# Loading q two groups ahead, and summing later key tiles on VectorE, in a fused attention and gate kernel

## The chip, the cores and the metric

The kernel runs on one core of one Trainium2 chip. The metric is the device time of one execution in microseconds (us). Three runs of the kernel before took 1133.68, 1138.77 and 1144.32 us; the median is 1138.77 us.

## The reference

Four batches (B = 4) of 12288 queries with C = 128 channels attend to 768 keys. The keys are a 4 x 4 mean over a 384 x 32 image, multiplied by `w_sr`; they serve as values too. The result goes through a five-tap causal convolution that makes a gate, and through two 128 x 128 products.

```
kv_pool = kv.reshape(B, H // r, r, W // r, r, C).mean(axis=(2, 4))     # r = 4
k = v = kv_pool.reshape(B, -1, C) @ w_sr                               # 768 keys a batch
a = softmax(q @ k.T / sqrt(C))                                         # 12288 x 768 a batch
x = a @ v
gate = sigmoid(sum over 5 taps of conv_w[k] * x shifted by 4 - k)
out = (gate * (x @ w_val)) @ w_out
```

## The kernel before

The 12288 queries of a batch are cut into 24 **groups** of 512 queries, 96 groups in all, and a group into 4 **steps** of 128 queries (j = 0 to 3). The schedule is written out by hand: one loop over all 384 steps emits, step by step, what each engine is to do, and each engine runs its instructions in that order. Work on a group is spread over several groups of the loop: at group gi the loop does the scores of gi (one step ahead), the product with the values ("AV") of gi - 2 (`avg`), the convolution of gi - 3 (`xg`) and the two last products of gi - 4 (`mg`).

What one step puts on each engine, with the lines of the profile:

- TensorE (PE): six matmuls of scores for the next step (L262); a part of the 18 AV matmuls of `avg` (L344), cut by `AV_CUTS`; at j = 0 the turning of the row sums (L290, into the tile `m`, of which there is one buffer); at j = 1 the product with `w_val` (L400, into `m` too); at j = 2 the product with `w_out` (L410); at j = 3 six transposes of the probabilities (L310), which need the tile `pf` from ScalarE.
- VectorE (DVE): the row maximum (L268), the low half of the probabilities of the step before (`p_lo`, L331); at j = 0 the reciprocal (L287); at j = 1 the copy `r` of the turned row sums (L297) and `h` (L405); at j = 3 `x` (L361), which scales AV by the row sums `rb`.
- ScalarE (ACT): the exponential (L280), the high half of the probabilities (L327), one tap of the convolution, a tanh, a copy out, and at j = 2 the rounded query `qh` (L244) of group gi + 2.
- GpSimd (POOL): the query's remainder `ql` (L248), four taps (L371) and four sums (L380) of the convolution.
- SyncE (SP) issues nearly all DMAs from one queue in order: the transposing DMAs that bring the probabilities of steps 0 to 2 from `hl` to `pt` (L335), the store `rd` (L298) and the broadcast load `rb` (L303) of the row sums, the query loads (L233), the output stores (L424).

The scores of a step lie in a pair of PSUM banks, `s`; there are three pairs, so the scores written at the end of a group (those for j = 0 of the next group) take the pair that `p_lo` of step j = 1 leaves.

Queries come in pairs of groups, into a tile `q` with two buffers. The pair gi + 2, gi + 3 is loaded at j = 0 of an even gi, and `qh` of gi + 2 is asked for at j = 2 of the same group.

Keys of the first batch come in 16 pieces of 48 keys (`load_kv`, L118) into `kvt`, and VectorE sums each (`pool_kv`, L123). The keys of the other batches are made while the batch before them is worked on, one small job a group (`setup_steps`, run at j = 3). There a half of the keys is 4 loads of 768 KB to the same tile, `rows`: a plain one from SP (L131) and three from GpSimd's queue that add to what is there (L133). VectorE then sums four neighbours in four instructions (`pool_rows`, L138), each in the group after its job, at j = 0, between `p_lo` and the next row maximum. Then come two projections, the scaling of the values and their splitting, in seven more jobs.

Of the kernel before, what the change touches and what calls it, by code (L numbers as in the profile page):

```python
# [6 lines left out]
F32 = mybir.dt.float32  # L7
F32R = mybir.dt.float32r
F16 = mybir.dt.float16
I32 = mybir.dt.int32  # L10
AF = mybir.ActivationFunctionType
ALU = mybir.AluOpType
AX = mybir.AxisListType
PSUM = bass.MemoryType.PSUM

R = 4
# [11 lines left out]
def attn_moe_kernel(ctx, tc, qT, kvT, w_sr, w_moe, outT):  # L28


    nc = tc.nc
    B, C, N = qT.shape
    NK, RR = kvT.shape[3] // R, R * R
    NCH = NK // P
    HALF = NK // 2
    NG = N // GQ
    NW = w_moe.shape[1]
    TAPS = NW - 2 * C
    HALO = TAPS - 1
    PIECES = 16  # L40
    AV_CUTS = (0, 7, 10, 14, 18)
    assert 3 * NCH == AV_CUTS[-1]
    PC = NK // PIECES
    QC = NK // 4
    scale = 1.0 / float(C) ** 0.5

    const = ctx.enter_context(tc.tile_pool(name="const", bufs=1))
    kvp = ctx.enter_context(tc.tile_pool(name="kvp", bufs=4))
# [25 lines left out]
    def load_moe():  # L74

        if w_moe.dtype == F32:
            nc.sync.dma_start(out=wm, in_=w_moe)
            return []
        raw = kvp.tile([C, HALF * R], F32, name="rows0", bufs=1).bitcast(I32)[:, :2 * NW]
        rest = kvp.tile([C, HALF * R], F32, name="rows1", bufs=1)  # L80
        nc.sync.dma_start(out=raw, in_=w_moe.bitcast(I32))
        words = raw.rearrange("c (n w) -> c w n", w=2)
        lo, hi = words[:, 0], words[:, 1]
        sign, ex, a, t = (rest.bitcast(I32)[:, i * NW:(i + 1) * NW] for i in range(4))
        low = rest[:, 4 * NW:5 * NW]
        v = nc.vector

        def two(out, in_, s1, op0, s2, op1):
            return lambda: v.tensor_scalar(out=out, in0=in_, scalar1=s1, scalar2=s2,
                                           op0=op0, op1=op1)  # L90

        def one(out, in_, s1, op):
            return lambda: v.tensor_single_scalar(out=out, in_=in_, scalar=s1, op=op)

        def both(out, x, y, op):
            return lambda: v.tensor_tensor(out=out, in0=x, in1=y, op=op)

        return [
            two(ex, hi, 20, ALU.logical_shift_right, 0x7FF, ALU.bitwise_and),
            two(ex, ex, -896.0, ALU.add, 0.0, ALU.max),  # L100
            two(ex, ex, 255.0, ALU.min, float(1 << 23), ALU.mult),
            two(a, hi, 0xFFFFF, ALU.bitwise_and, 3, ALU.logical_shift_left),
            two(t, lo, 29, ALU.logical_shift_right, 7, ALU.bitwise_and),
            both(a, a, t, ALU.bitwise_or),
            one(a, a, 0x3F800000, ALU.bitwise_or),
            one(sign, hi, -2147483648, ALU.bitwise_and),
            both(a, a, sign, ALU.bitwise_or),
            one(t, lo, 0x1FFFFFFF, ALU.bitwise_and),
            two(low, t, 2.0 ** -52, ALU.mult, 0.0, ALU.add),
            both(low.bitcast(I32), low.bitcast(I32), sign, ALU.bitwise_or),  # L110
            both(low, low, a.bitcast(F32), ALU.add),
            both(wm, low, ex.bitcast(F32), ALU.mult),
        ]

    def load_kv(st, i):
        t = kvp.tile([C, R, PC * R], F32, name="kvt", bufs=5)
        src = kvT[0].rearrange("r c x -> c r x")
        nc.sync.dma_start(out=t, in_=src[:, :, i * PC * R:(i + 1) * PC * R])  # L118
        st["kv", i] = t

    def pool_kv(st, i):
        t = st.pop(("kv", i))
        nc.vector.tensor_reduce(out=st["pool"][:, i * PC:(i + 1) * PC],  # L123
                                in_=t.rearrange("c r (k s) -> c k r s", s=R),
                                axis=AX.XY, op=ALU.add)

    def load_rows(b, st, h, r):
        src = kvT[b, r, :, h * HALF * R:(h + 1) * HALF * R]
        if r == 0:
            st["rows", h] = kvp.tile([C, HALF * R], F32, name=f"rows{h}", bufs=1)  # L130
            nc.sync.dma_start(out=st["rows", h], in_=src)  # L131
        else:
            nc.gpsimd.dma_start(out=st["rows", h], in_=src, accum_op=ALU.add)  # L133

    def pool_rows(st, i):
        t = st["rows", i // 2].rearrange("c (k s) -> c k s", s=R)
        k0 = i % 2 * QC
        nc.vector.tensor_reduce(out=st["pool"][:, i * QC:(i + 1) * QC], in_=t[:, k0:k0 + QC],  # L138
                                axis=AX.X, op=ALU.add)

    def key_tiles(st):
        st["pool"] = keys.tile([C, NK], F32, name="pool", bufs=1)
        for n in ("kh", "kl"):
            st[n] = keys.tile([C, NK], F32R, name=n)
        for n in ("vh", "vl"):
            st[n] = keys.tile([P, NK], F16, name=n)
        st["vt"] = keys.tile([C, NK], F32, name="vt", bufs=1)
# [67 lines left out]
                lambda: values(st, 1, misc()) or split_values(st, 1)]  # L215

    def setup_steps(b, st):
        loads = [(h, r) for r in range(1, R) for h in range(2)]
        steps = [lambda: key_tiles(st) or load_rows(b, st, 0, 0) or load_rows(b, st, 1, 0)]
        for h, r in loads:  # L220
            steps += [lambda: None, lambda h=h, r=r: load_rows(b, st, h, r)]
        steps += [lambda i=i: (None, lambda: pool_rows(st, i)) for i in range(4)]
        steps += [lambda h=h: project(st, h, misc()) or split_keys(st, h) for h in range(2)]
        return steps + value_steps(st)

# [214 lines left out]
    def at(i):  # L440
        return groups[i] if 0 <= i < G else None

    ctx.enter_context(tc.manual_schedule())
    st = states[0]
    key_tiles(st)
    for i in range(5):
        load_kv(st, i)
    load_second = load_pair(at(0), at(1), parts=2)
    nc.sync.dma_start(out=wsr, in_=w_sr)
    g_qh(at(0))  # L450
    g_ql(at(0))
    low = None
    for i in range(PIECES):
        if i + 5 < PIECES:
            load_kv(st, i + 5)
        if i == 3:
            convert = load_moe()
        pool_kv(st, i)
        if i >= 8 and convert:
            convert.pop(0)()  # L460
        if i == 3 * PIECES // 4:
            low()
        if i % (PIECES // 2) == PIECES // 2 - 1:
            h = 2 * i // PIECES
            project(st, h, bank_pair()[:, 0])
            high, low = split_keys(st, h)
            high()
    low()
    load_second()
    score(at(0), 0)  # L470
    g_qh(at(1))
    g_ql(at(1))

    steps = value_steps(st)
# [6 lines left out]
    for t in range(NT * G):  # L481
        gi, j = divmod(t, NT)
        cur, prev, nxt = (at(u // NT) for u in (t, t - 1, t + 1))
        last, avg, xg, mg, og = (at(gi - d) for d in (1, 2, 3, 4, 5))
        if j == 0 and gi % 2 == 0 and at(gi + 2):
            load_pair(at(gi + 2), at(gi + 3))
        if gi % NG == 1 and j == 0 and at(gi + NG - 1):
            steps += setup_steps(cur.b + 1, states[cur.b + 1])
        if t == NT + 2:
            trickle += convert  # L490

        if nxt:
            score(nxt, (j + 1) % NT)
        if mg and j == 1:
            mg.m = g_val(mg, misc())
        if mg and j == 2:
            mg.m = g_out(mg.h, misc())
        if avg:
            av_part(avg, j)

        if high and (j == 0 or t < NT):
            high()
            high = None
        row_max(cur, j)
        expo(cur, j)
        if on_pe(j):
            turn(cur, j)
            norm_eps(cur)
            if mg:
                out_tile(mg)  # L510
                g_evac(mg, mg.m)
        p_hi(cur, j)
        if mg and j == 0:
            mg.th = g_tanh(mg.gate)
        if xg and j == 1:
            tap(xg, TAPS - 1, nc.scalar)
        if last and j == 0:
            norm_reciprocal(last)
        if last and j == 1:
            norm_store(last)  # L520
        drip()
        if prev:
            p_lo(prev, (j - 1) % NT)
        if low and (j == 0 or t < NT):
            low()
            low = None
        if last and j == 0:
            norm_turn(last, misc())
        drip()
        if mg and j == 1:  # L530
            mg.h = g_h(mg.th, mg.m)
        if avg and j == 3:
            new_x(avg, xg, nc.gpsimd.tensor_copy)
            g_x(avg, avg.av)
        if xg and j == 1:
            g_conv(xg)
        if last and j == 3:
            norm_rows(last)
        if at(gi + 2) and j == 2:
            g_qh(at(gi + 2))  # L540
            g_ql(at(gi + 2))
        if og and j == 0 and og.i % 2:
            store_pair(og)
        if steps and (j == 3 or t < NT):
            high, low = steps.pop(0)() or (None, None)
# [83 lines left out]
```

## Time and profile before

| | |
|---|---|
| median of three runs | 1138.77 us (1133.68 to 1144.32) |
| the profiled execution's own time | 1141.0 us |
| its span, first to last instruction | 1139.2 us |
| granted TensorE clock, mean | 0.992 |
| busy: PE, DVE, ACT, POOL | 1059.9, 895.8, 909.0, 879.5 us |
| DMA queues' packets, share of 16 engines | q1 (from SP) 83.6%, q0 (from GpSimd) 7.7% |

The span is what the trace covers; the 1.8 us around it belong to the execution's own time. In rows of the profile, `out<-in` names the tiles, `x` the number of instructions, and what stands in brackets is the idle time of that engine just before, with the instruction that ended it. "L310 x6" are the six transposes at the end of a group, so the time from one such row to the next is the time of one group. "PEld" is TensorE's weight load, "SPq" an instruction of the SP queue. A busy PE is counted from modelled ends of pipelined matmuls: busy time there isn't time in which nothing more would fit.

### The profile page before, as it was taken

What the parts mean: (1) busy time and instruction counts of PE and PEld (TensorE: products, weight loads), DVE (VectorE), ACT (ScalarE), POOL (GpSimd) and SP (SyncE); (2) the same over time, 40 slices, a digit from 0 to 9 for tenths busy, and PEclk for the clock granted to TensorE, in tenths of its full rate; (3) what the DMA queues carried; (4) which work ended last, traced back from release to release, by engine and by line L of the source; (5) the groups of instructions that cost most, each with busy time, mean ns of one, the idle gap of its engine ahead of it and who ended that gap; (6) DMA issues with size and microseconds to landing.
All of it is one profiled execution on the core that took longest, in us unless ns stands there. A gap on an engine that the chain in (4) does not pass through costs nothing.

```text
span 1139.2 us, 16531 instructions
## 1 busy us (share of the span) xinstructions
PE 1059.9 (93%) x5174; PEld 711.9 (62%) x5174; DVE 895.8 (79%) x1254; ACT 909.0 (80%) x1659; POOL 879.5 (77%) x966
## 2 busy tenths in 40 slices
PE   1889999999999989999999999899999999999996
PEld 0656666666666656666666666566666666666663
DVE  6877777888877767788888787688887888778784
ACT  1777888888887878788888788788888888888882
POOL 0178888888878878887888898788887888888872
PEclk9999999999999999999999999999999999999999
DMA  8599999998989999989879999999798888878973
GB/s 269 99 229 186 213 195 229 187 181 184 188 200 203 219 178 204 197 180 190 177 161 226 226 212 216 178 210 185 155 176 191 176 172 193 189 160 183 197 148 107
DMA packets 489783, 215.53 MB, mean 189 GB/s; under 512 B 452704, under 2 KB 461664, under 8 KB 489696
## 3 DMA queue, kind: packets, MB, share of 16 engines
q1 hardware_dynamic: 487104, 200.32, 83.6%
q0 software_dynamic: 2592, 14.16, 7.7%
q8 instruction: 41, 0.67, 0.2%
q14 instruction: 46, 0.38, 0.1%
HBM read 75.83 MB, written 25.36 MB: 89 GB/s over the span
## 4 chain that ended last, share of the span: by engine, by line
PE 39%; DMA 23%; DVE 13%; ACT 12%; POOL 8%; issue 3%; SPq 2%; DVEq 0%; ACTq 0%; POOLq 0%
DMA q<-in_q 16%; PE s L262 14%; PE av L344 13%; DMA rb<-rd 6%; PE m L400 5%; DVE nm L268 5%; POOL tap L371 4%; PE s L310 4%; POOL ql L248 3%; ACT qh L244 3%; ACT s L280 3%; DVE x L361 3%; ACT pf L280 3%; ACT hl L327 2%; PE m L410 2%
## 5 line engine op out<-in xcount | busy, mean ns | idle before, releaser
L380 POOL TENSOR_TENSOR sum<-sum,tap 128x512 f32<-128x512 f32 x282 | 359.6, 1275 | 22.1
L344 PE MATMUL av<-pt,vh 128*128 128x512 f16 x1140 | 359.7, 384 | 9.3 <-DVE x L361 9.3
L268 DVE TENSOR_REDUCE nm<-s 128x1 f32<-128x768 f32 x384 | 364.3, 949 | 2.6 <-PE s L262 2.5
L280 ACT ACTIVATE s<-s,nm 128x768 f32<-128x768 f32 x288 | 251.5, 873 | 108.2 <-PE s L262 71.0
L371 POOL TENSOR_SCALAR tap<-x,wm 128x512 f32<-128x512 f32 x376 | 257.5, 738 | 64.8 <-DVE x L361 62.2
L331 DVE SCALAR_TENSOR_TENSOR hl<-s,hl 128x768 f16<-128x768 f32 x288 | 273.3, 949 | 22.4 <-ACT hl L327 21.4
L262 PE MATMUL s<-kh,qh 128*128 128x384 f32 x768 | 252.6, 410 | 4.2 <-DVE pw L181 2.5
L327 ACT ACTIVATE hl<-s 128x768 f16<-128x768 f32 x288 | 233.6, 811 | 9.1
L248 POOL TENSOR_TENSOR ql<-q,qh 128x512 fp32r<-128x512 f32 x96 | 121.7, 1268 | 152.2 <-ACT qh L244 148.3
L344 PE MATMUL av<-pt,vl 128*128 128x512 f16 x570 | 217.5, 382 | 0.0
L344 PEld LDWEIGHTS <-vh 128*128 128x128 f16 x1164 | 106.8, 98 | 175.5 <-issue 97.5
L262 PE MATMUL s<-kl,qh 128*128 128x384 f32 x768 | 198.3, 339 | 0.0
L262 PE MATMUL s<-kh,ql 128*128 128x384 f32 x768 | 198.1, 339 | 0.0
L262 PEld LDWEIGHTS s<-kh,qh 128*128 128x128 f32 x768 | 132.3, 192 | 44.3 <-issue 3.2
L361 DVE SCALAR_TENSOR_TENSOR x<-av,down,rb 128x512 f32<-128x512 f32 x95 | 71.3, 751 | 97.3 <-PE av L344 36.9
L262 PEld LDWEIGHTS s<-kl,qh 128*128 128x128 f32 x768 | 140.3, 189 | 0.5 <-DVE kl L163 0.5
L262 PEld LDWEIGHTS s<-kh,ql 128*128 128x128 f32 x768 | 140.5, 189 | 0.0
L380 POOL TENSOR_TENSOR sum<-tap,tap 128x512 f32<-128x512 f32 x94 | 124.2, 1321 | 0.0
L405 DVE SCALAR_TENSOR_TENSOR h<-th,m 128x512 f32<-128x512 f32 x94 | 64.7, 688 | 69.7 <-PE m L400 65.4
L344 PEld LDWEIGHTS <-vl 128*128 128x128 f16 x582 | 57.1, 98 | 86.9 <-issue 53.4
L331 DVE SCALAR_TENSOR_TENSOR pt<-s,pt 128x768 f16<-128x768 f32 x96 | 90.3, 940 | 24.4 <-ACT pt L327 24.1
L310 PE MATMUL s<-ident,pf 128*128 128x128 f32 x576 | 81.1, 277 | 27.8 <-ACT pf L280 27.5
(68 smaller groups left out, 1056.0 us busy)
## 6 DMA issues: line engine op xcount, KB each, us to landing
rb<-rd SPq DMA_DIRECT2D x96, 256.0 KB, 5.0
q<-in_q SPq DMA_DIRECT2D x47, 512.0 KB, 6.3
out<-o SPq DMA_DIRECT2D x46, 512.0 KB, 6.8
rows<-in_kv POOLq DMA_DIRECT2D x18, 768.0 KB, 7.5
kvt<-in_kv SPq DMA_DIRECT2D x16, 384.0 KB, 5.5
rows<-in_kv SPq DMA_DIRECT2D x6, 768.0 KB
pt<-hl SPq DMA_TRANSPOSE x192, 5.7
rd<-r SPq DMA_DIRECT2D x96, 2.0 KB
```

Of the source, the lines that this page charges most:

```text
L248: nc.gpsimd.tensor_tensor(out=g.ql, in0=g.q, in1=g.qh.bitcast(F32), op=ALU.subtract)
L262: nc.tensor.matmul(s[:, h, :HALF], a[:, sl], k[:, h * HALF:(h + 1) * HALF], start=(i == 0), stop=(i == 2))
L268: nc.vector.tensor_reduce(out=nm, in_=g.s[j], axis=AX.XY, op=ALU.max, negate=True)
L280: nc.scalar.activation(out=halves(g.pf[j]) if on_pe(j) else g.s[j], in_=g.s[j], func=AF.Exp, bias=g.nm.pop(j), accum_out=g.z[:, j:j + 1])
L310: nc.tensor.transpose(g.s[j][:, k // (NCH // 2), c:c + P], pf[:, k * P:(k + 1) * P], ident)
L327: nc.scalar.activation(out=part(g, j, 0), in_=g.s[j], func=AF.Copy, scale=2.0 ** 15)
L331: nc.vector.scalar_tensor_tensor(out=part(g, j, 1), in0=g.s.pop(j), scalar=2.0 ** 15, in1=part(g, j, 0), op0=ALU.mult, op1=ALU.subtract)
L344: nc.tensor.matmul(out, g.st[v][:, k * P:(k + 1) * P], g.pt[:, j0:j1, a * NCH + k], start=(i == 0), stop=(i == len(AV_ORDER) - 1))
L361: nc.vector.scalar_tensor_tensor(out=g.x[:, HALO + c0:HALO + c1], in0=av, scalar=g.st["down"], in1=g.rb[:, c0:c1], op0=ALU.mult, op1=ALU.mult)
L371: eng.tensor_scalar(out=g.tap[k], in0=src, scalar1=w, scalar2=1.0, op0=ALU.mult, op1=ALU.mult)
L380: nc.gpsimd.tensor_tensor(out=s, in0=acc, in1=g.tap[k], op=ALU.add)
L405: nc.vector.scalar_tensor_tensor(out=h, in0=th, scalar=1.0, in1=m, op0=ALU.add, op1=ALU.mult)
```

## The change

The change has four parts.

1. The query pair gi + 4, gi + 5 is loaded at j = 2 of an even gi, where before the pair gi + 2, gi + 3 was loaded at j = 0. The pair of groups 2 and 3 is loaded ahead of the loop.
2. Keys of later batches come in 16 plain loads of 384 KB a batch from SP, one a group (three in the first), into the same five buffers `kvt`; VectorE sums 16 neighbours of a piece in one instruction, one a group, at the place where `pool_rows` stood. The adding DMAs from GpSimd are gone, and the jobs of a batch are 23 where they were 24.
3. The host lays the 16 neighbours of a key side by side, so that a partition's share of a piece is one run of 3072 bytes, where it was four of 768 bytes. This holds for the first batch too.
4. The 18 AV matmuls of a group are cut 7, 2, 3, 6 over the four steps; before they were cut 7, 3, 4, 4.

```
-    AV_CUTS = (0, 7, 10, 14, 18)
+    AV_CUTS = (0, 7, 9, 12, 18)
...
-    def load_rows(b, st, h, r):
-        src = kvT[b, r, :, h * HALF * R:(h + 1) * HALF * R]
-        if r == 0:
-            st["rows", h] = kvp.tile([C, HALF * R], F32, name=f"rows{h}", bufs=1)
-            nc.sync.dma_start(out=st["rows", h], in_=src)
-        else:
-            nc.gpsimd.dma_start(out=st["rows", h], in_=src, accum_op=ALU.add)
+    def load_kv(b, st, i):
+        st["kv", i] = kvp.tile([C, PC * RR], F32, name="kvt", bufs=AHEAD)      # AHEAD = 5
+        nc.sync.dma_start(out=st["kv", i], in_=kvT[b, :, i * PC * RR:(i + 1) * PC * RR])
...
-                                in_=t.rearrange("c r (k s) -> c k r s", s=R),
-                                axis=AX.XY, op=ALU.add)
+                                in_=st.pop(("kv", i)).rearrange("c (k s) -> c k s", s=RR),
+                                axis=AX.X, op=ALU.add)
...
     def setup_steps(b, st):
-        loads = [(h, r) for r in range(1, R) for h in range(2)]
-        steps = [lambda: key_tiles(st) or load_rows(b, st, 0, 0) or load_rows(b, st, 1, 0)]
-        for h, r in loads:
-            steps += [lambda: None, lambda h=h, r=r: load_rows(b, st, h, r)]
-        steps += [lambda i=i: (None, lambda: pool_rows(st, i)) for i in range(4)]
+        def piece(i):
+            if i == 0:
+                key_tiles(st)
+            for k in range(3) if i == 0 else (i + 2,):
+                if k < PIECES:
+                    load_kv(b, st, k)
+            return None, lambda: pool_kv(st, i)
+
+        steps = [lambda i=i: piece(i) for i in range(PIECES)]
...
     low()
     load_second()
+    load_pair(at(2), at(3))
     score(at(0), 0)
...
-        if j == 0 and gi % 2 == 0 and at(gi + 2):
-            load_pair(at(gi + 2), at(gi + 3))
+        if j == 2 and gi % 2 == 0 and at(gi + 4):
+            load_pair(at(gi + 4), at(gi + 5))
```

The SP queue over two groups of the loop, before, where no key is loaded (each row is one DMA; `q` is the query pair, `rd` and `rb` the row sums, `pt<-hl` the transposes):

```order
L233 DMA q<-in_q 128x1024
L424 DMA out<-o 128x1024
L298 DMA rd<-r 4x128
L335 DMA_TRANSPOSE pt<-hl 128x24x128
L335 DMA_TRANSPOSE pt<-hl 128x12x128
L303 DMA rb<-rd 128x512
L298 DMA rd<-r 4x128
L335 DMA_TRANSPOSE pt<-hl 128x24x128
L335 DMA_TRANSPOSE pt<-hl 128x12x128
L303 DMA rb<-rd 128x512
```

The same queue after the change, where a piece of keys is loaded in every group:

```order
L412 DMA out<-o 128x1024
L286 DMA rd<-r 4x128
L221 DMA q<-in_q 128x1024
L323 DMA_TRANSPOSE pt<-hl 128x24x128
L323 DMA_TRANSPOSE pt<-hl 128x12x128
L291 DMA rb<-rd 128x512
L118 DMA kvt<-in_kv 128x768
L286 DMA rd<-r 4x128
L323 DMA_TRANSPOSE pt<-hl 128x24x128
L323 DMA_TRANSPOSE pt<-hl 128x12x128
L291 DMA rb<-rd 128x512
L118 DMA kvt<-in_kv 128x768
```

`q` stood behind `rb` and ahead of `rd`; now it stands behind `rd` and ahead of the two transposes, half a group later in the order but for a pair that is needed two groups further on. A load of keys has come in behind each `rb`.

VectorE's row in a group of such a stretch, before (from `x` of one group on):

```order
L361 SCALAR_TENSOR_TENSOR x<-av,down,rb 128x512
L268 TENSOR_REDUCE nm<-s 128x1
L287 RECIPROCAL z_102<-z_102 128x4
L331 SCALAR_TENSOR_TENSOR pt<-s,pt 128x768
L268 TENSOR_REDUCE nm<-s 128x1
L297 COPY r<-m 4x128
L331 SCALAR_TENSOR_TENSOR hl<-s,hl 128x768
L405 SCALAR_TENSOR_TENSOR h<-th,m 128x512
L268 TENSOR_REDUCE nm<-s 128x1
L331 SCALAR_TENSOR_TENSOR hl<-s,hl 128x768
L268 TENSOR_REDUCE nm<-s 128x1
L331 SCALAR_TENSOR_TENSOR hl<-s,hl 128x768
```

And after the change:

```order
L349 SCALAR_TENSOR_TENSOR x<-av,down,rb 128x512
L256 TENSOR_REDUCE nm<-s 128x1
L275 RECIPROCAL z_102<-z_102 128x4
L319 SCALAR_TENSOR_TENSOR pt<-s,pt 128x768
L121 TENSOR_REDUCE pool<-kvt 128x48
L256 TENSOR_REDUCE nm<-s 128x1
L285 COPY r<-m 4x128
L319 SCALAR_TENSOR_TENSOR hl<-s,hl 128x768
L393 SCALAR_TENSOR_TENSOR h<-th,m 128x512
L256 TENSOR_REDUCE nm<-s 128x1
L319 SCALAR_TENSOR_TENSOR hl<-s,hl 128x768
L256 TENSOR_REDUCE nm<-s 128x1
```

One sum of keys has come in ahead of the row maximum of j = 1, of `r` and of `h`, in 16 groups of each of three batches; before there was such an instruction in 4 groups of each.

More of the change, by code (lines that the diff above doesn't have):

```diff
@@ L32, in attn_moe_kernel @@
     B, C, N = qT.shape
-    NK, RR = kvT.shape[3] // R, R * R
+    RR = R * R
+    NK = kvT.shape[2] // RR
     NCH = NK // P
@@ L40, in attn_moe_kernel @@
     PIECES = 16
-    AV_CUTS = (0, 7, 10, 14, 18)
+    AV_CUTS = (0, 7, 9, 12, 18)
     assert 3 * NCH == AV_CUTS[-1]
     PC = NK // PIECES
-    QC = NK // 4
+    AHEAD = 5
     scale = 1.0 / float(C) ** 0.5
@@ L78, in load_moe @@
             return []
-        raw = kvp.tile([C, HALF * R], F32, name="rows0", bufs=1).bitcast(I32)[:, :2 * NW]
-        rest = kvp.tile([C, HALF * R], F32, name="rows1", bufs=1)
+        raw = kvp.tile([C, 2 * NW], I32, name="raw", bufs=1)
+        rest = kvp.tile([C, 5 * NW], F32, name="rest", bufs=1)
         nc.sync.dma_start(out=raw, in_=w_moe.bitcast(I32))
@@ L113, in load_moe @@
         ]
[L115 to L119, printed above, removed]
+    def load_kv(b, st, i):
+        st["kv", i] = kvp.tile([C, PC * RR], F32, name="kvt", bufs=AHEAD)
+        nc.sync.dma_start(out=st["kv", i], in_=kvT[b, :, i * PC * RR:(i + 1) * PC * RR])
     def pool_kv(st, i):
-        t = st.pop(("kv", i))
         nc.vector.tensor_reduce(out=st["pool"][:, i * PC:(i + 1) * PC],
-                                in_=t.rearrange("c r (k s) -> c k r s", s=R),
-                                axis=AX.XY, op=ALU.add)
-    def load_rows(b, st, h, r):
-        src = kvT[b, r, :, h * HALF * R:(h + 1) * HALF * R]
-        if r == 0:
-            st["rows", h] = kvp.tile([C, HALF * R], F32, name=f"rows{h}", bufs=1)
-            nc.sync.dma_start(out=st["rows", h], in_=src)
-        else:
[L133 to L138, printed above, removed]
+                                in_=st.pop(("kv", i)).rearrange("c (k s) -> c k s", s=RR),
                                 axis=AX.X, op=ALU.add)
@@ L445, in attn_moe_kernel @@
     key_tiles(st)
-    for i in range(5):
-        load_kv(st, i)
+    for i in range(AHEAD):
+        load_kv(0, st, i)
     load_second = load_pair(at(0), at(1), parts=2)
@@ L453, in attn_moe_kernel @@
     for i in range(PIECES):
-        if i + 5 < PIECES:
-            load_kv(st, i + 5)
+        if i + AHEAD < PIECES:
+            load_kv(0, st, i + AHEAD)
         if i == 3:
@@ L615 @@
         "in_kv": np.ascontiguousarray(
-            kv.reshape(B, H // R, R, W // R, R, C).transpose(0, 2, 5, 1, 3, 4)
-        ).reshape(B, R, C, -1),
+            kv.reshape(B, H // R, R, W // R, R, C).transpose(0, 5, 1, 3, 2, 4)
+        ).reshape(B, C, -1),
         "in_w_sr": np.ascontiguousarray(w_sr),
```

## The prediction

> **What bounds the kernel now.** I read the page first: the busy times and the chain that ended last.
>
> ```profile
> span 1139.2 us, 16531 instructions
> PE 1059.9 (93%) x5174; PEld 711.9 (62%) x5174; DVE 895.8 (79%) x1254; ACT 909.0 (80%) x1659; POOL 879.5 (77%) x966
> PE 39%; DMA 23%; DVE 13%; ACT 12%; POOL 8%; issue 3%; SPq 2%; DVEq 0%; ACTq 0%; POOLq 0%
> DMA q<-in_q 16%; PE s L262 14%; PE av L344 13%; DMA rb<-rd 6%; PE m L400 5%; DVE nm L268 5%; POOL tap L371 4%; PE s L310 4%; POOL ql L248 3%; ACT qh L244 3%; ACT s L280 3%; DVE x L361 3%; ACT pf L280 3%; ACT hl L327 2%; PE m L410 2%
> ```
>
> TensorE is busiest, yet the load of q makes up 16% of the chain. A share of the chain is no gain: what runs beside the load may be just behind it. So I read the chain in order of time in a quiet stretch (no keys are loaded there), and the timeline beside it.
>
> ```profile
> 1025.40 2.43 POOL tap L371 x4
> 1027.84 5.89 DMA q<-in_q
> ...
> 1033.75 0.62 ACT qh L244
> 1034.37 0.91 ACT pf L280 x2
> ...
> 1035.32 0.87 PE s L310 x6
> ...
> 1037.24 1.53 PE av L344 x7
> ```
>
> ```profile
> 1026.94 0.85 SPq L303 DMA_DIRECT2D rb<-rd  x1
> 1027.84 0.43 SPq L233 DMA_DIRECT2D q<-in_q  x1
> ...
> 1035.32 0.87 PE L310 MATMUL s<-ident,pf 128*128 128x128 f32 x6 [0.34 <-ACT pf L280]
> ...
> 1045.98 0.82 PE L310 MATMUL s<-ident,pf 128*128 128x128 f32 x6
> ```
>
> The load is issued when SP has issued `rb`, lands 5.9 us later, and ScalarE can't make `qh`, nor `pf` behind it in its queue, before; TensorE's transposes wait 0.34 us for `pf`. The next group has no new load: it takes 45.98 - 35.32 = 10.66 us and TensorE doesn't wait. So TensorE is the bound just below the wait for q. How long groups are, stage by stage, is read from the transposes alone (six a group), in a table by stage: its columns are the stretch, its length, PE's and PEld's busy time with counts, the granted clock, the DMA share and GB/s.
>
> ```profile
> 60.71:240.98 180.27, 13.61 (x96) 10.77 (x96) 0.99 1.01 205
> 319.28:506.74 187.46, 13.49 (x96) 10.91 (x97) 0.99 1.03 202
> 597.14:780.73 183.59, 13.43 (x96) 10.98 (x97) 0.99 1.03 207
> 882.35:1100.43 218.08, 16.98 (x120) 13.60 (x121) 1.00 0.85 179
> 1079.14:1100.43 21.29, 1.69 (x12) 1.50 (x13) 1.00 0.83 165
> ...
> 218.76:251.99 33.23, 2.57 (x18) 2.13 (x19) 1.00 0.81 165
> 495.72:528.91 33.19, 2.57 (x18) 2.13 (x19) 1.00 0.78 165
> 769.69:802.92 33.23, 2.57 (x18) 2.11 (x19) 1.00 0.81 165
> ...
> 240.98:319.28 78.30, 5.90 (x42) 4.91 (x43) 1.00 0.82 172
> 506.74:597.14 90.40, 6.78 (x48) 5.41 (x48) 1.00 0.86 175
> 780.73:882.35 101.62, 7.48 (x54) 6.12 (x54) 1.00 0.86 180
> 39.90:60.71 20.81, 1.75 (x12) 1.27 (x12) 1.00 0.95 170
> ```
>
> Rows 1 to 3 are the three **key stretches**: the 16 groups each in which, after the change, a piece of keys is summed. They take 551.3 us, 11.49 a group, and the DMA engines are full (1.01 to 1.03). Row 4 is the quiet end, 20 groups of 10.90. Row 5 is its last two groups, behind the last load of q: 10.65 a group, which I take as the **floor** of a group. Rows 6 to 8 are three groups each in which VectorE sums keys: 11.07 a group. Rows 9 to 11 are the 24 groups in which keys are projected and split, with the quiet ones between; row 12 is groups 1 and 2.
>
> **The change, part by part.** What q and its neighbours cost as waits over the whole run (total, times, longest):
>
> ```profile
> ACT qh L244 <- DMA q<-in_q: 42.6, 36, 9.6
> DVE x L361 <- DMA rb<-rd: 20.2, 7, 5.3
> PEld m L400 <- DVE r L297: 7.9, 13, 1.9
> ```
>
> *q two groups ahead.* After the change a pair is issued behind `rd` of an even group and used two groups, some 21 us, later; the load takes 5.9 us. ScalarE's 42.6 us of waits go, but for the first (9.6 us, in the start). The buffer it takes was last read by `ql` of the next group, which GpSimd finishes a group before SP gets there, so SP isn't held, and the transposes queued behind it aren't. What is late next is TensorE itself: in the quiet end 20 groups fall from 218.1 to 20 x 10.65 = 213.0, **-5.1 us**.
>
> *Keys by plain loads, summed by VectorE.* What stands in the trace for the instructions:
>
> ```profile
> L123 DVE TENSOR_REDUCE pool<-kvt 128x48 f32<-128x768 f32 x16 | 15.2, 952 | 8.3 <-DMA kvt<-in_kv 8.3
> L138 DVE TENSOR_REDUCE pool<-rows 128x192 f32<-128x768 f32 x12 | 11.3, 943 | 0.0
> L133 POOL DMA_DIRECT2D rows<-in_kv x18 | 16.0, 889 | 0.0
> q0 software_dynamic: 2592, 14.16, 7.7%
> ```
>
> Gone are 18 issues of 0.89 us on GpSimd and 12 sums of 0.94 us on VectorE; new are 48 sums of 0.95 us, 45.7 us for 11.3. VectorE has the room (79% busy), but not at every place. The timeline of a group with a sum shows it:
>
> ```profile
> 487.02 0.94 DVE L138 TENSOR_REDUCE pool<-rows 128x192 f32<-128x768 f32 x1
> ...
> 488.75 0.27 DVE L297 COPY r<-m 4x128 f32<-4x128 f32 x1
> ...
> 489.07 1.12 PE L400 MATMUL m<-x,wm 128*128 128x512 f32 x2 [0.29 <-DVE r L297]
> ...
> 491.78 0.95 DVE L331 SCALAR_TENSOR_TENSOR hl<-s,hl 128x768 f16<-128x768 f32 x1
> ...
> 493.26 0.70 PE L262 MATMUL s<-kh,qh 128*128 128x384 f32 x2
> ```
>
> The sum makes `r` late, `r` holds the one buffer `m`, and TensorE waits 0.29 us ahead of the product with `w_val`. The rest of the 0.95 us fits into VectorE's own idle time. The nine groups of rows 6 to 8 hold one such sum each and no key load, and some of them a wait for q: 11.07 us is their time, 0.42 above the floor. I take it for all 48: 48 x 11.07 = 531.4 for 551.3, **-19.9 us**. The bounds are 10.65 (the sum hides, -40.1) and 11.60 (floor and the whole 0.95, +5.5).
>
> This needs the DMA engines to have room. The adding loads took 7.7% of 1139.2 us, 87.7 us of all sixteen engines, for 18 x 768 KB: 2.4 us for each 384 KB. No row shows a load in runs of 3072 bytes. Below it can't cost less than nothing, above no more than the adding one, 2.4 us a group. As adding also reads what is there, a plain load should need half, 1.2 us, and I take that. On top of a share of 0.80 in rows 6 to 8 that is 0.80 + 1.2 / 11.07 = 0.91, below the full engines of before; at 2.4 us it would be 1.02, as before. SP's own issue of a piece, behind `rb`, falls into time in which SP waits for VectorE.
>
> The Trainium skill, VectorE: DVE Perf Modes, section Rules for kernel authors, speaks against this part: a `tensor_reduce` on a hot path runs in the slowest mode, and one should restructure to avoid it. The trace agrees on the pace (952 ns for 768 elements); by the rule taken whole the 48 sums would lie on the path, which is the third rival below.
>
> *Seven jobs of projecting and splitting* stay, a group earlier. Rows 9 to 11 give 270.3 us for 24 groups, 14.7 above the floor. Half of the groups wait for q as in the quiet end (0.5 us a pair, 12 pairs, would be 6); as the jobs also hold TensorE there, I take 4: **-4 us** (0 to -8). Groups 1 and 2 take 20.81; the second stands behind a load of q, and I take **-1.4 us**, down to 9.7 a group (0 to -2).
>
> *The start.* Pieces of the first batch come as runs of 3072 bytes where they were 768. VectorE waits 8.3 us for them in all (the row of L123 above), part of that for the very first piece, and from the middle on VectorE's own work paces it. Between 0 and 8.3 I take **-2 us**, nearer to zero for that reason.
>
> *AV 7, 2, 3, 6.* Seven AV matmuls take 1.53 us in the chain above, 0.22 each. All 18 still end at the same place ahead of the transposes, and so do `x` and the transposes; only the scores of j = 3 come 0.22 us earlier and those of the next j = 0 come 0.44 earlier. What follows them isn't waiting for them: VectorE makes `x` first. So I take **0**. But cover is lost: the scores at 493.26 need the banks that `p_lo` leaves at 491.78 + 0.95 = 492.73. Of 0.53 us, 0.09 remain.
>
> **Sum**: -5.1 - 19.9 - 4 - 1.4 - 2 = -32.4 us. The profiled execution took 1141.0 us (span 1139.2), so 1108.6; it lay 2.2 us above the median of its three runs, and against that median I say **1106 us**, 2.9% less.
>
> **The rivals.**
>
> *Sums hidden.* Now that no load of q delays ScalarE, VectorE could run ahead and `r` come in time: 48 x 0.42 = 20 us more, 1086. Against it: at 487.02 the sum starts as soon as `p_lo` is done, and what it follows (`x`) is tied to the end of AV, so VectorE can't run ahead. Chance 0.10.
>
> *The DMA engines stay full.* The bytes of keys are the same, and all now stand in SP's queue with the transposes. If a plain load costs as much as the adding one, `rb` stays late as often: its 20.2 us of waits remain, in key stretches that also carry the sums. 1106 + 20 = 1126. For it: a share of 1.01 to 1.03 there. Against it: the estimate of 0.91. Chance 0.10.
>
> *VectorE paces the key stretches.* Each sum whole on the path, 11.60 a group: 556.8 for 531.4, 1106 + 25 = 1131, no measurable difference. Against it: rows 6 to 8. Chance 0.06.
>
> *Slower: the score banks.* `p_lo` of j = 1 comes later than now by what VectorE is behind, and since the cuts leave 0.09 us of cover, TensorE waits for the banks in every group with a sum. If the sum's full 0.95 us reached that place, 48 x (0.95 - 0.09) = 41 us: 1147. It decides against the change from 32.4 / 48 = 0.68 us of such a wait a group. Against it: in the row of 491.78 the sum has passed, and 0.53 us were left. Chance 0.04.
>
> **How the numbers follow.** The forecast has 0.70, with 1094 to 1120 about it (the bounds of the small terms, and 10.8 to 11.3 a group in the key stretches). With the rivals at 1126 and part of the one at 1086, the range for 8 in 10 is 1090 to 1126. About 1% (11 us) is what a measurement of this kernel can tell from no change. Faster by over 1% means below 1127.4: the forecast, the first rival and nearly all of the second, 0.87. Within 1%: the third and half of the fourth, with some of the second, 0.09. Slower by over 1%: the rest of the fourth and what I haven't thought of, 0.04.
>
> **What the profile will show.** If I am right: no wait of `qh` for q beyond the first; groups at the quiet end of 10.65 each, odd and even alike; about 11.07 in the key stretches, with 48 waits of the `w_val` product for `r` in place of 13; a DMA share near 0.9 there and no wait for `rb`; less than 8.3 us of waits for the first pieces. I am wrong if scores (L262) wait for `p_lo` (L331) group after group, if `rb` still holds `x`, or if the quiet end stays at 10.9 with another wait in front of `pf`.

## The result, and the profile after

The changed kernel takes **1131.45 us** (median of 11 runs, 1129.39 to 1133.22); the kernel before, run beside it and counted together with its first three runs, takes 1143.97 us (median of 11). The ratio is **0.9906** (95% interval 0.9879 to 0.9933): about 1% faster. The ratio is worked out from fast runs alone, so it isn't the quotient of the two medians. The forecast was 1106 us, with a range from 1090 to 1126, so the change gave a third of what was forecast and the range missed the time. The profiled execution took 1133.22 us with a span of 1131.4.

The page of the changed kernel, its first two lines, the chain and the DMA queue of SP:

```profile
span 1131.4 us, 16595 instructions
PE 1063.6 (94%) x5174; PEld 715.6 (63%) x5174; DVE 919.0 (81%) x1290; ACT 910.4 (80%) x1659; POOL 864.4 (76%) x948
...
PE 49%; DVE 25%; ACT 11%; issue 6%; POOL 5%; DMA 3%; SPq 1%; DVEq 0%; ACTq 0%
PE s L250 17%; PE av L332 16%; PE m L388 8%; DVE nm L256 8%; POOL ql L236 5%; ACT s L268 5%; DVE pool L121 4%; DVE pt L319 4%; ACT hl L315 4%; DVE x L349 4%; PE m L398 3%; PE s L298 3%; DMA kvt<-in_kv 3%; ACT qh L232 2%; DVE h L393 2%
...
q1 hardware_dynamic: 487008, 214.48, 85.4%
```

The load of q, 16% of the chain before, is gone from it. A new item stands there with 3%: the load of keys, `kvt<-in_kv`. The waits of the changed kernel (total, times, longest) tell where:

```profile
PEld m L388 <- DVE r L285: 40.3, 48, 7.7
...
DVE pool L121 <- DMA kvt<-in_kv: 25.2, 8, 7.0
...
ACT qh L232 <- DMA q<-in_q: 7.8, 1, 7.8
```

`qh` waits for q once, in the start. But VectorE now waits for key pieces, up to 7.0 us at a time: three of the eight waits are over 6 us, one in each key stretch, and the other five, 5.4 us together, lie in the start. The table by stage, by the transposes (L298 here), takes the key stretches apart into their first group and the other 15, with the quiet end in the fourth row:

```profile
73.35:239.55 166.20, 12.27 (x90) 10.68 (x90) 1.00 0.94 208
337.38:503.68 166.30, 12.28 (x90) 10.71 (x90) 1.00 0.93 204
613.15:779.41 166.26, 12.28 (x90) 10.70 (x90) 1.00 0.92 204
878.39:1090.87 212.48, 16.42 (x120) 14.28 (x121) 1.00 0.85 182
56.09:73.35 17.26, 0.82 (x6) 0.72 (x6) 0.80 0.71 167
317.29:337.38 20.09, 0.82 (x6) 0.73 (x7) 0.83 0.83 197
592.01:613.15 21.14, 0.82 (x6) 0.73 (x7) 0.76 0.80 195
```

Fifteen groups take 166.3 us, 11.08 each, and the quiet end 10.62 each: both are what the forecast has. The first group of each key stretch takes 17.26, 20.09 and 21.14 us, together 58.5 for 3 x 11.08 = 33.2. These **25.3 us in three groups** are what is missing. The timeline of the second one shows how:

```profile
314.71 5.11 SPq L323 DMA_TRANSPOSE pt<-hl  x2
319.87 0.87 SPq L291 DMA_DIRECT2D rb<-rd  x1
320.79 1.38 SPq L118 DMA_DIRECT2D kvt<-in_kv  x3
...
326.78 0.95 DVE L121 TENSOR_REDUCE pool<-kvt 128x48 f32<-128x768 f32 x1 [6.67 <-DMA kvt<-in_kv]
327.65 0.95 DVE L256 TENSOR_REDUCE nm<-s 128x1 f32<-128x768 f32 x1
328.52 0.27 DVE L285 COPY r<-m 4x128 f32<-4x128 f32 x1
...
328.84 2.08 PE L388 MATMUL m<-x,wm 128*128 128x512 f32 x2 [6.97 <-DVE r L285]
```

In the first job of a batch the program loads three pieces and, at the very next step, sums the first. The load stands in SP's queue behind the transposes and `rb`, so SP issues it at 320.79, while VectorE has been waiting since 326.78 - 6.67 = 320.11. It gets the piece 6 us after the issue. Everything in VectorE's row stands behind the sum: the row maximum, `r`, and through `r` the product with `w_val` on TensorE. On top of that the clock falls: its mean in the three long groups is 0.76 to 0.83, and the two matmuls of L388 take 2.08 us, where the same two take 1.02 in a kernel shown further down that doesn't stall. The Trainium skill, TensorE: Matmul & The Clock Gate, Part 1: The HAM clock gate, says that TensorE drops to half of its clock after an idle window of about 3.4 us. The trace agrees: TensorE had been idle for 6.97 us ahead of that row, and the matmuls in it take twice as long.

### The profile page after: what moved, and what is told of

It is laid out like the page before. It is cut to its first block, busy times and chain, and to the rows that moved or that the text cites. A ratio compares the mean times of both kernels' runs of the same rounds, so it can differ in the third digit from the quotient of the medians.

```text
span 1131.4 us, 16595 instructions
## 1 busy us (share of the span) xinstructions
PE 1063.6 (94%) x5174; PEld 715.6 (63%) x5174; DVE 919.0 (81%) x1290; ACT 910.4 (80%) x1659; POOL 864.4 (76%) x948
## 4 chain that ended last, share of the span: by engine, by line
PE 49%; DVE 25%; ACT 11%; issue 6%; POOL 5%; DMA 3%; SPq 1%; DVEq 0%; ACTq 0%
PE s L250 17%; PE av L332 16%; PE m L388 8%; DVE nm L256 8%; POOL ql L236 5%; ACT s L268 5%; DVE pool L121 4%; DVE pt L319 4%; ACT hl L315 4%; DVE x L349 4%; PE m L398 3%; PE s L298 3%; DMA kvt<-in_kv 3%; ACT qh L232 2%; DVE h L393 2%
## 5 line engine op out<-in xcount | busy, mean ns | idle before, releaser
L332 PE MATMUL av<-pt,vh 128*128 128x512 f16 x1140 | 389.1, 383 | 0.0
L359 POOL TENSOR_SCALAR tap<-x,wm 128x512 f32<-128x512 f32 x376 | 253.4, 693 | 82.4 <-DVE x L349 80.9
L332 PEld LDWEIGHTS <-vh 128*128 128x128 f16 x1164 | 114.0, 98 | 175.5 <-issue 85.8
L388 PE MATMUL m<-x,wm 128*128 128x512 f32 x188 | 103.0, 630 | 25.0 <-DVE r L285 24.9
L368 POOL TENSOR_TENSOR sum<-tap,tap 128x512 f32<-128x512 f32 x94 | 120.4, 1281 | 0.0
L315 ACT ACTIVATE pt<-s 128x768 f16<-128x768 f32 x96 | 77.8, 810 | 37.8 <-PE s L298 37.8
```

Of the source, the lines that this page charges most:

```text
L315: nc.scalar.activation(out=part(g, j, 0), in_=g.s[j], func=AF.Copy, scale=2.0 ** 15)
L332: nc.tensor.matmul(out, g.st[v][:, k * P:(k + 1) * P], g.pt[:, j0:j1, a * NCH + k], start=(i == 0), stop=(i == len(AV_ORDER) - 1))
L359: eng.tensor_scalar(out=g.tap[k], in0=src, scalar1=w, scalar2=1.0, op0=ALU.mult, op1=ALU.mult)
L368: nc.gpsimd.tensor_tensor(out=s, in0=acc, in1=g.tap[k], op=ALU.add)
L388: nc.tensor.matmul(m, wval, g.x[:, HALO + c0:HALO + c1], start=True, stop=True)
```

## The experiments

### One group later for every sum

```
-            return None, lambda: pool_kv(st, i)
+            return (None, lambda: pool_kv(st, i - 1)) if i else None

-        steps = [lambda i=i: piece(i) for i in range(PIECES)]
+        steps = [lambda i=i: piece(i) for i in range(PIECES + 1)]
```

> The changed kernel, with each piece of keys summed one job (one group) later than now; loads stay where they are. Theory: the 25 us that are missing against the forecast are the first group of each key stretch (17.3, 20.1 and 21.1 us where its neighbours take 11.1), because VectorE asks for the first piece when SP, behind the transposes and rb, has not issued its load or has only just done so. Then these three groups take 11.1 us and the kernel 1106 us (ratio 0.967). Rival: the DMA engines are what lacks in these groups; then the wait turns up at another tile (rb, pt) and the time stays near 1131 us (0.99).

It took 1106.29 us (6 runs, 1105.22 to 1107.83), ratio 0.9699 (0.9661 to 0.9738). The first row is the group in which the second key stretch begins in the changed kernel (there the 20.09 of above), the second the 16 groups behind it, the third the quiet end:

```profile
310.01:321.33 11.32, 0.82 (x6) 0.72 (x7) 1.00 0.92 221
321.33:498.35 177.02, 13.10 (x96) 11.47 (x97) 1.00 0.96 214
852.95:1065.42 212.47, 16.42 (x120) 14.28 (x121) 1.00 0.84 181
```

No long group is left. One of the 16 groups holds no sum now; at the quiet 10.6 for that one, the other 15 take (177.02 - 10.6) / 15 = 11.09 us each. The wait turned up nowhere else: VectorE's waits for key pieces are down to 5.5 us, all in the start, and no wait for `rb` or `pt` has come up. One thing the edit does besides: with one more job a batch, the jobs of the second and third batch begin a group or two later, and their loads with them. The lead from a piece's load to its sum is longer by one group all the same (in the second batch the load is issued at 324.89 and the sum starts at 334.68). The theory holds and its rival falls. The 25 us are shown to be the missing lead between a load and its sum.

### The other end: the first loads earlier

```
         def piece(i):
-            if i == 0:
-                key_tiles(st)
-            for k in range(3) if i == 0 else (i + 2,):
-                if k < PIECES:
-                    load_kv(b, st, k)
+            if 0 < i < PIECES - 2:
+                load_kv(b, st, i + 2)
...
         if gi % NG == 1 and j == 0 and at(gi + NG - 1):
+            key_tiles(states[cur.b + 1])
+            for k in range(3):
+                load_kv(cur.b + 1, states[cur.b + 1], k)
             steps += setup_steps(cur.b + 1, states[cur.b + 1])
```

> The changed kernel with sums where they are, and the first three pieces of a batch issued at j = 0 of the group in which its jobs are put on the list, three steps ahead of the first job and so ahead of that group's transposes. Theory: it is the lead from a piece's issue to its sum that was short, whichever end is moved; the three long groups go to 11.1 us and the kernel to 1106 us (0.97). Rival: three loads at a time hold up rb or pt wherever they stand, or three pieces in one burst land late anyway: 1120 to 1131 us (0.98 to 0.99).

It took 1107.31 us (6 runs), ratio 0.9646 (0.9608 to 0.9685). The group with the first sum of the second batch, and the 15 behind it:

```profile
309.57:320.64 11.07, 0.82 (x6) 0.71 (x7) 1.00 1.03 223
320.64:486.77 166.13, 12.28 (x90) 10.66 (x91) 1.00 0.94 207
```

So the burst of three loads by itself does no harm. Whichever end is moved, the three long groups go (in this trace they take 10.13, 11.07 and 11.10 us).

### AV cut as before

```
-    AV_CUTS = (0, 7, 9, 12, 18)
+    AV_CUTS = (0, 7, 10, 14, 18)
```

> The changed kernel with AV cut 7, 3, 4, 4 as before. Theory: the cuts move only scores that nobody waits for: 1131 us, no difference from the changed kernel (within 3 us). Rival: the cuts 7, 2, 3, 6 lose cover at the score banks, and the old ones are 5 us or more faster; or they hide something, and the old ones are 5 us or more slower.

It took 1132.09 us (11 runs, 1131.02 to 1133.10), ratio 0.9917 (0.9890 to 0.9944), beside 1131.45 us with the new cuts. Long group, the 15 behind it, quiet end:

```profile
317.98:338.32 20.34, 0.82 (x6) 0.73 (x7) 0.75 0.81 200
338.32:504.61 166.29, 12.27 (x90) 10.74 (x90) 1.00 0.91 203
877.88:1090.10 212.22, 16.42 (x120) 14.21 (x121) 1.00 0.87 182
```

Each is within 0.3 us of its row in the changed kernel. The cuts neither gain nor lose, and the score banks, the rival on the slower side, hold nobody up.

### q alone, and keys alone

The first is the kernel before with the two edits of `load_pair` only; the second is the changed kernel without them and with the old cuts.

> The kernel before, with q alone loaded two groups ahead (keys by adding DMAs, AV cut as before). Theory: outside of the key stretches the gain is that of the changed kernel (about 12 us); in the key stretches the waits for q go and those for rb stay, 540 us for 551: 1120 us in all (0.979). Rival: the adding loads fill the DMA engines, so that what q no longer waits turns up at rb and pt, and the key stretches stay at 551 us: 1131 us (0.99).

> The changed kernel with q loaded as before and AV cut as before: the keys' part alone. Theory: 48 sums at 11.1 us a group, half a microsecond a pair for q, and three first groups that wait for their piece, 25 us: key stretches of about 569 us for 551, a start that is 3 us shorter, 1159 us in all (1.013). Rival: it was the adding DMAs that made q and rb late, and without them the key stretches shrink although q is loaded late: 1131 us or less (0.99).

q alone took 1111.35 us (6 runs), ratio **0.9745** (0.9705 to 0.9786), better than the 1120 of its theory. Keys alone took 1164.59 us (6 runs), ratio **1.0205** (1.0157 to 1.0252): slower than before, as expected, but by more than the 1159 us of its theory. From the trace of q alone, the stretch of the second batch's keys and the quiet end; then the wait for `rb`:

```profile
310.60:489.79 179.19, 13.10 (x96) 11.43 (x97) 1.00 1.04 212
857.46:1069.81 212.35, 16.42 (x120) 14.26 (x120) 1.00 0.86 181
```

```profile
DVE x L361 <- DMA rb<-rd: 43.3, 20, 3.4
```

Its key stretch takes 179.19 us for 187.46 before, although the DMA share with the adding loads is still 1.04 and `rb` comes late more often than before (20 times for 7). I had 540 us for the three stretches and the trace has 533.2. From the trace of keys alone, the long group, the 15 behind it and the quiet end, and its waits:

```profile
329.86:349.41 19.55, 0.82 (x6) 0.73 (x7) 0.83 0.78 200
349.41:522.88 173.47, 12.62 (x90) 10.23 (x90) 1.00 0.91 195
908.92:1126.67 217.75, 16.99 (x120) 13.61 (x121) 1.00 0.85 180
```

```profile
ACT qh L232 <- DMA q<-in_q: 46.7, 36, 7.9
```

Without adding loads (share 0.91) the groups behind the long one still take 11.56 us: q waits as much as in the kernel before, 46.7 us for 42.6. So it wasn't contention that made q late, but its place in the order. The three stretches take 581.6 us in this trace, where I had 569: I took half a microsecond a pair for the late q, and in these stretches most pairs have a group of 12.0 to 13.3 us beside one of 11.0. In medians: from 1141.49 us (the kernel before, run beside these) q alone reaches 1111.35, a gain of 30 us, and with the keys part on top of it the kernel stands at 1132.09 (old cuts) or 1131.45 (new ones), so 20 us are given back. With the sums one group later the two parts together take 1106.29 us. So without the stall the keys part is worth 5 us on top of q, half of it in the start: the first transposes come at 37.30 us for 39.80 with q alone.

### The sum at another place in VectorE's row

With the sums one group later, a group with a sum still takes 11.08 us for 10.61. The forecast put that down to `r`. Two kernels, shown here against the one with the sums one group later, move the sum behind `r`, one just ahead of `h` (j = 1), one just ahead of `x` (j = 3). `kv_sum` is a list that the job fills:

```
-            return (None, lambda: pool_kv(st, i - 1)) if i else None
+            return kv_sum.append(lambda: pool_kv(st, i - 1)) if i else None
...
+        if kv_sum and j == 1:              # the other kernel: j == 3, ahead of new_x and g_x
+            kv_sum.pop(0)()
         if mg and j == 1:
             mg.h = g_h(mg.th, mg.m)
```

> The kernel with the pieces summed one group later, with the sum moved down VectorE's row: from j = 0 (ahead of a row maximum and r) to j = 1, just ahead of h, where VectorE sits idle 0.85 us in a group without a sum. Theory: a sum costs TensorE 0.47 us a group (11.08 for 10.61) only because it makes r late, and r holds the one buffer m; then key groups take 10.6 to 10.75 and the kernel 1086 to 1092 us (ratio 0.952). Rival: VectorE has no room for it anywhere (it paces the key groups); then h and the maxima behind it come late by as much, and the time stays at 1106 us (0.97).

> As the kernel with the sum just ahead of h, but the sum at j = 3, just ahead of x, where VectorE waits 0.9 us for the end of AV. Theory: the sum fits into that wait, x is late by 0.1 us at most, and key groups take 10.6 to 10.7: 1085 to 1090 us (0.95). Rival as there: VectorE paces the key groups, 1106 us (0.97).

They took 1082.43 us (6 runs, 1082.09 to 1083.57), ratio **0.9434** (0.9397 to 0.9471), and 1083.69 us, ratio 0.9448 (0.9407 to 0.9490). The first lies a little below the 1086 to 1092 us of its theory, the second below its 1085 to 1090. From the trace of the first, busy times of PE, PEld, DVE, ACT and POOL in the second batch's key stretch, and VectorE's timeline around the sum, with one row of TensorE:

```profile
312.65:482.46 169.81, 169.81 (x849) 116.78 (x849) 151.42 (x207) 149.23 (x274) 146.70 (x161) 1.00 1.01 223
```

```profile
422.38 0.27 DVE L286 COPY r<-m 4x128 f32<-4x128 f32 x1
422.58 0.95 DVE L320 SCALAR_TENSOR_TENSOR hl<-s,hl 128x768 f16<-128x768 f32 x1
423.20 1.02 PE L389 MATMUL m<-x,wm 128*128 128x512 f32 x2
423.45 0.94 DVE L121 TENSOR_REDUCE pool<-kvt 128x48 f32<-128x768 f32 x1
424.33 0.69 DVE L394 SCALAR_TENSOR_TENSOR h<-th,m 128x512 f32<-128x512 f32 x1
```

16 groups, 15 of them with a sum, take 169.81 us, 10.61 each, as the quiet end's do (10.62 in the changed kernel), and PE's busy time is the whole stretch. The sum fills the time in which `h` waited for the product with `w_val`. The sum costs nothing where it stands behind `r`; ahead of `r` it cost 0.47 us a group. VectorE's pace was never the reason. The waits of TensorE for `r` say the same, first with the sums one group later, then with the sum ahead of `h`:

```profile
PEld m L388 <- DVE r L285: 26.8, 49, 1.9
```

```profile
PEld m L389 <- DVE r L286: 1.9, 1, 1.9
```

Forty-eight of these waits go, 24.9 us in all, and the medians differ by 23.9. That it is the one buffer `m` through which a late `r` holds TensorE is read from the program; a kernel with two such buffers wasn't run. Both versions beat the kernel before and the changed one.

## Why the prediction was wrong

By its own steps, from the two profiled executions. The bounds of the stages after stand in the table by stage above: projecting and splitting lies between the key stretches (239.55 to 317.29, 503.68 to 592.01, 779.41 to 878.39), in all 265.05 us for 270.32, and the end from 1090.87 on. Groups 1 and 2 of the changed kernel, from its first transposes:

```profile
36.89:56.09 19.20, 1.75 (x12) 1.42 (x13) 1.00 0.93 168
```

| step | forecast, us | trace, us |
|---|---|---|
| quiet end | -5.1 | -5.6 |
| key stretches | -19.9 | **+5.9** |
| projecting and splitting | -4 | -5.3 |
| groups 1 and 2 | -1.4 | -1.6 |
| start, to the first transposes | -2 | -3.0 |
| end, from the last transposes | 0 | +1.8 |
| sum of span | -32.4 | -7.8 |

The medians differ by 12.5 us, not 7.8: the profiled execution of the kernel before lies 3 us below its median, that of the changed kernel 1.8 us above.

**The step that failed** is the second edit, "keys by plain loads, summed by VectorE". It said that SP's own issue of a piece "falls into time in which SP waits for VectorE", and took 11.07 us for all 48 groups. For 45 of them this was right to 0.01 us. It never asked when a piece *lands*: the first of a batch is asked for in the step after its load is issued, and VectorE's row behind it, which the text lists for `r`, then waits too. That is 25.3 us in three groups. It was to be seen: the diff loads and sums piece 0 in one job, the row of `pool<-kvt` that it quotes has VectorE waiting 8.3 us for the same tile in the start, and the section on what a wait has queued behind it was written for q alone. None of the rivals had this mechanism; without it the time is the forecast's, as 1106.29 us show. That it agrees so closely is in part luck: start, projecting and splitting gained 2.3 us more than forecast and the end lost 1.8, and the forecast was set against a median of 1138.77 us, where the kernel before took 1141.49 beside this run.

The working also books the gain under the wrong part. Nearly all of the -19.9 that stands under the keys is q's: with q alone the three stretches fall from 551.3 to 533.2 us. The working left open how much of the 11.49 us a group was q's and how much the adding loads'; q alone reaches 11.11 with the adding loads still there.

**Right, and shown**: the floor of a group (10.65 forecast, 10.61), the end of q's waits, the cost of a sum at its place and its cause (a late `r`), no effect of the cuts, and a DMA share below 1 (0.91 forecast, 0.92 to 0.94). The estimate of 1.2 us for a plain piece was near: in the trace its 128 packets of 3072 bytes take 137 ns each in the mean, 1.1 us of all sixteen engines.

**Of the rivals**, "sums hidden" didn't happen, though it could be had by another place in the row. "VectorE paces the key stretches" is refuted by the moved sum. Its time, 1131 us, is the measured one, but by chance: it spreads 25 us over 48 groups of 11.60, and the trace has them in three groups, with 11.08 in the other 45. With this rival falls the rule taken whole that the working sets beside it. The Trainium skill, VectorE: DVE Perf Modes, Rules for kernel authors, says to expect 1x of a `tensor_reduce` on a hot path, as the slowest of VectorE's operations, and to consider restructuring. The trace has 0.94 us a piece for it, and that cost nothing at one place and 0.47 us a group at another. "The DMA engines stay full" had the share wrong and, more than that, its price.

The end is 1.8 us longer in the profiled execution. The last AV of the chain, before and then after (start, length, what, matmuls):

```profile
1114.47 3.90 PE av L344 x18
```

```profile
1104.91 5.59 PE av L332 x18
```

Its 18 matmuls take 1.69 us more, nearly the whole of it. Six us that hold most of them, before and then after; the third figure from the end is the granted clock:

```profile
1112.00:1118.00 6.00, 4.66 (x20) 2.08 (x21) 1.83 (x3) 1.32 (x4) 5.76 (x7) 1.00 0.99 237
```

```profile
1102.50:1108.50 6.00, 4.72 (x12) 1.80 (x13) 1.83 (x3) 1.26 (x4) 5.76 (x7) 0.72 0.92 234
```

So the clock was lower there, 0.72 for 1.00. Why it was is open. It isn't the new cuts (the end takes 40.2 us with the old ones, 40.5 with the new) nor the change as a whole (38.9 with the sum ahead of `h`, 38.8 in the kernel before).

## What to carry to other kernels

A load that is moved into a queue needs two prices: what its issue takes, and how long before its first use it can have landed; look at the first of a series by itself, since a pipeline that runs ahead by two pieces runs ahead by none at its first. An instruction added to an engine with idle time to spare costs by its place: ahead of what holds a single buffer it cost 0.47 us, behind it nothing. Parts of a change that are priced together should be read apart too: here one part gained 30 us and the other gave 20 of them back. And a time that agrees with a rival doesn't make the rival right: 1131 us was also the time of "VectorE paces the key stretches", and only the groups one by one told the two apart.

## What the hardware showed that I had not expected

A DMA share of 1.0 wasn't a bound here. With the sum ahead of `h` the key stretch runs at a share of 1.01 and 223 GB/s, more than the 202 GB/s at 1.03 of the kernel before, and TensorE's row has no gap; with q alone it is 1.04 and 11.20 us a group, with waits for `rb`. So the share doesn't tell the two apart. I had read 1.01 to 1.03 as full engines. The Trainium skill, Perfetto Trace Analysis, section Identifying the Most-Contended Engine, says that sixteen engines make their occupancy misleading. These rows agree.

A stall of 6 to 7 us cost more than itself. The other two first sums of the changed kernel:

```profile
64.92 0.95 DVE L121 TENSOR_REDUCE pool<-kvt 128x48 f32<-128x768 f32 x1 [6.07 <-DMA kvt<-in_kv]
601.86 0.95 DVE L121 TENSOR_REDUCE pool<-kvt 128x48 f32<-128x768 f32 x1 [7.03 <-DMA kvt<-in_kv]
```

With the 6.67 shown above VectorE waited 19.8 us in all, and the three groups lost 25.3, with the clock at 0.76 to 0.83 of its full rate. By these means the three groups had 17.26 x 0.20 + 20.09 x 0.17 + 21.14 x 0.24 = 11.9 us less of full clock. Some of that falls into the idling itself, so it is an upper estimate of what the clock added; the missing 5.5 us lie within it.
